# Delta rule with a gated MLP: the state's products woven in pairs, U and S in buffers of their own

## The chip, the cores and the metric

The kernel runs on one core of one Trainium2 chip. The metric is the device time of one execution in microseconds (us); before the change it is 664.31 us, the median of three runs that went from 662.4 to 664.77 us. A difference of less than about 0.5% (3.3 us) can't be told from no change.

## The reference

What is computed, cut to what matters: a linear attention with a state per head, updated token by token by the delta rule, and a spatially gated MLP behind it.

```python
k_n = k / (np.linalg.norm(k, axis=-1, keepdims=True) + 1e-06)
for t in range(S):                       # S = 768; B, H, D = 4, 8, 48
    kt, vt, bt = (k_n[:, :, t], v[:, :, t], beta[:, :, t, None])
    y[:, :, t] = np.einsum('bhd,bhde->bhe', q[:, :, t], state)
    v_old = np.einsum('bhde,bhd->bhe', state, kt)
    state = state + bt[:, :, :, None] * np.einsum('bhd,bhe->bhde', kt, vt - v_old)
...
h = np.maximum(x @ w_in, 0.0)            # x: y as (4, 768, 384); d_ff = 1024
u, v = (h[..., :d_ff // 2], h[..., d_ff // 2:])
v_n = (v - mu) / np.sqrt(var + 1e-06)    # over the last axis
v_s = np.einsum('ts,bsd->btd', w_spatial, v_n) + b_spatial[None, :, None]
return ((u * v_s) @ w_out).astype(np.float32)
```

All matrix products are in float32 or in pairs of rounded halves (`float32r`).

## The kernel before

The sequence of each batch is cut into 12 chunks of 64 tokens. One **step** handles one chunk of one batch with its 8 heads; there are 48 steps. Head h + 2u stands with h = 0 or 1 on one half of the 128 partitions and with u = 0 to 3 along the free axis. Two chains of steps (batches 0 and 2, batches 1 and 3) are interleaved by the list `ORDER`: six steps of the first chain alone, then one of each in turn, then six of the second alone. A step whose chain is also that of the step before it (`late`) is called `solo` in the code.

In each step these groups of small matrix products run on TensorE (8 calls each, 4 u by 2 h; every float32 call shows in the trace as two weight loads and two matmuls):

- **products** (line 359): K times K and K times Q of a later chunk; two VectorE operations (lines 373 and 374) mask them into `ta`. Both use K padded with zeros to 128 rows, so that a call has 128 rows and 64 columns and streams 128 columns. There is one such call group for each of the steps 8 to 47.
- **E** (line 585) and **F** (line 597): the lower left 32 by 32 block of the inverse of a unit triangular matrix, 32 rows by 32 columns, on the diagonal halves of the array (input and output on the same half of the partitions). ScalarE copies the results (lines 588 and 600, one copy for each h). The inverses of the 32 by 32 blocks come from "lanes" (lines 531 to 566), a long chain of VectorE operations for each group of 4 steps.
- **A** (line 642): K times the state S; VectorE adds it to v (line 645). Its operands lie on the half opposite to that of the result.
- **B** (line 659): the inverse times v; VectorE scales it into U, one operation for each h (line 663).
- **C** (line 678): K natural times U; VectorE adds it to S, one operation for each h (line 682).
- **D** (line 692): the output, from S and U in one call of 112 or 128 rows and 64 columns. For this, S and U of a head stand in one buffer `su`, S on one half of the partitions and U on the other, and ScalarE copies the masked K times Q (line 650, `step_k`) beside Q into `kqa`, so that both are one operand.

The groups of a step are issued in three places: `slot_a` (A and F of step s), `slot_cd` (C and D of step `late`, the step before), `slot_b` (B of s, E of s + 1). In each place lie, behind the groups, the products of later steps, some VectorE operations of the lanes (`lane`), pieces of the preparation of weights and norms (`pump`) and `fill(rate)`, which issues matmuls of the MLP worth `rate` us (1.5, from step 18 on 1.7) up to a cap. The groups are issued under a higher priority (`hp()`, 300 instructions ahead). The order on each engine but VectorE in the opening is then found by the tile framework's scheduler, which goes by priority and by when operands are ready and buffers free; PSUM buffers for A to F come from one pool, `pa`, with four.

The MLP (lines 752 to 896) takes products of 128 rows by 128 columns: `mlp_v` (line 759), `mlp_u` (820), `mlp_g` (839), `mlp_o` (884). What is left of it when the steps are over runs at the end by itself.

SyncE issues all DMAs, among them per step `kqa` in two parts (lines 622 and 623), `knat` (617), `v` (612) and the padded `kq` (336).

Of the kernel before, what the change touches and what calls it, by code (L numbers as in the profile page):

```python
# [15 lines left out]
CH = 64  # L16
# [62 lines left out]
def delta_rule_gated_mlp(  # L79
# [3 lines left out]
    kp_t: bass.AP,  # L83
    qb_t: bass.AP,
    qa_t: bass.AP,
    kv_nat: bass.AP,
    b_nat: bass.AP,
# [39 lines left out]
    sus = []  # L127
    for i in range(4):
        su = const.tile([128, 2 * NU * HD + 16], F32, name=f"su{i}")
        nc.gpsimd.memset(su, 0.0)  # L130
        sus.append(su)

    def su_view(t, h, u, rows, w=HD):
        o = (h * NU + u) * HD
        return t[rows, o : o + w]

    def su_all(t, h, rows):
        o = h * NU * HD
        return t[rows, o : o + NU * HD].rearrange("p (u e) -> p u e", e=HD)
# [131 lines left out]
    cn_g, ta_g, ad_g, w_g = {}, {}, {}, {}  # L271

    def group_norm(g):
# [49 lines left out]
        cn_g[g] = cn  # L323
# [3 lines left out]
    def load_kq(s):  # L327
        if s < NST:
            if KQB <= s < 2 * G:
                kq_t_[s] = moe.tile([KR, 2, NU, CH], F32, name="kq", tag="vh", bufs=VB)  # L330
            else:
                kq_t_[s] = work.tile([128, 3, NU, CH], F32, name="kq", bufs=KQB)
            if s < 2 * G:
                nc.sync.dma_start(out=kq_t_[s][0:KR, 0:2], in_=kq_t[s])
            else:
                nc.sync.dma_start(out=kq_t_[s], in_=kp_t[s - 2 * G])
# [11 lines left out]
    def products_mm(s):  # L348
# [7 lines left out]
        p1 = pq.tile([128, 512], F32, name="pq").rearrange("p (u y t) -> p u y t", u=NU, y=2)  # L356
        for u in range(NU):
            for h in range(2):
                nc.tensor.matmul(  # L359
                    p1[rows_t(h), u],  # L360
                    kq[:, h, u, :],
                    kq[:, h : 3 : 2 - h, u, :],
                    start=True,
                    stop=True,
                )
# [4 lines left out]
    def products_out(s, p1):  # L370
        g, sl = divmod(s, G)
        ta = ta_g[g]
        nv.tensor_tensor(out=ta[:, 0, sl], in0=p1[:, :, 0], in1=mcs[s % len(mcs)], op=ALU.mult)
        nv.tensor_tensor(
            out=ta[:, 1, sl], in0=p1[:, :, 1], in1=mpos.unsqueeze(1).broadcast_to([128, NU, CH]), op=ALU.mult
# [201 lines left out]
    def step_e(s):  # L577
        tt, tn = t_of(s), tn_t.pop(s)
        pi = pi_t[s] = work.tile([128, NU, 32], F32, name="pi", bufs=1)
        p2 = pa.tile([128, 512], F32, name="pa")  # L580
        pp = p2[:, : NU * 32].rearrange("p (u c) -> p u c", c=32)
        for u in range(NU):
            for h in range(2):
                r, lo = slice(h * 64, h * 64 + 32), slice(h * 64 + 32, h * 64 + 64)
                nc.tensor.matmul(pp[lo, u], tt[r, u, 32:64], tn[r, u, :], start=True, stop=True)
        for h in range(2):
            lo = slice(h * 64 + 32, h * 64 + 64)
            nc.scalar.copy(out=pi[lo], in_=pp[lo])

    def step_f(s):  # L590
        tt, pi = t_of(s), pi_t.pop(s)
        p3 = pa.tile([128, 512], F32, name="pa")
        px = p3[:, : NU * 32].rearrange("p (u c) -> p u c", c=32)
        for u in range(NU):
            for h in range(2):
                r, lo = slice(h * 64, h * 64 + 32), slice(h * 64 + 32, h * 64 + 64)
                nc.tensor.matmul(px[r, u], pi[lo, u, :], tt[lo, u, 32:64], start=True, stop=True)  # L597
        for h in range(2):
            r = slice(h * 64, h * 64 + 32)
            nc.scalar.copy(out=tt[r, :, 32:64], in_=px[r])  # L600
# [13 lines left out]
    def prefetch_kn(s):  # L614
        if s < NST:
            kn_t[s] = work.tile([128, NU, HD], F32, name="knat", bufs=2)
            nc.sync.dma_start(out=kn_t[s], in_=kv_nat[s, :, 0])

    def prefetch_kq(s):
        if s < NST:  # L620
            kqa = kqa_t[s] = work.tile([128, 3, NU, CH], F32, name="kqa", bufs=2)
            nc.sync.dma_start(out=kqa[0:64, 0:2], in_=qb_t[s])
            nc.sync.dma_start(out=kqa[64:112, 1:3], in_=qa_t[s])

    def step_v(s):
# [5 lines left out]
        if c == 0:  # L631
            nc.gpsimd.memset(sus[2 * ch], 0.0)

    def step_a(s):
        ch, b, c = ORDER[s]
        v, kqa, su = v_t[s], kqa_t[s], sus[2 * ch + c % 2]
        if c == 0:
            return
        pr = psl(pa.tile([128, 512], F32, name="pa"), HD)
        for u in range(NU):  # L640
            for h in range(2):
                nc.tensor.matmul(  # L642
                    pr[rows_t(h), u], kqa[rows_d(h), 1, u, :], su_view(su, h, u, rows_d(h)), start=True, stop=True
                )
        nc.vector.tensor_add(out=v, in0=v, in1=pr)  # L645

    def step_k(s):
        aqk, kqa = t_of(s, 1), kqa_t[s]
        for h in range(2):
            nc.scalar.copy(out=kqa[rows_t(h), 2 - 2 * h], in_=aqk[rows_t(h)])  # L650

    def step_b(s):
        ch, b, c = ORDER[s]
        tt, cn = t_of(s), cn_g[s // G][:, s % G]
        r, su = v_t.pop(s), sus[2 * ch + c % 2]
        pu = psl(pa.tile([128, 512], F32, name="pa"), HD)
        for u in range(NU):
            for h in range(2):
                mark["pb"] = nc.tensor.matmul(  # L659
# [608 lines left out]
```

## Time and profile before

| | |
|---|---|
| median of 3 runs | 664.31 us (662.4 to 664.77) |
| the profiled execution: first to last instruction | 665.8 us |
| TensorE: matmuls / weight loads busy | 564.1 us (85%) / 490.7 us (74%) |
| VectorE / ScalarE / GpSimd busy | 449.3 / 264.3 / 205.0 us |
| mean granted clock of TensorE | 0.885 |
| bytes moved by DMA | 74.63 MB |

The profile has one execution. Its span is 665.8 us, 1.5 us above the median of the runs; no separate time of that execution is given. PE is TensorE's matmuls and PEld its weight loads, which overlap; DVE is VectorE, ACT ScalarE, POOL GpSimd, SPq the queue that issues DMAs. A form such as `48*64 48x48` means weights of 48 rows by 64 columns, and a moving operand of 48 rows by 48 columns. In rows of the timeline, the first number is the start and the second the length of a merged run of instructions, both in us, and xN their number.

### The profile page before, as it was taken

How to read it: one execution, taken by the hardware profiler on the slowest of the kernel's cores; microseconds unless marked ns; L12 is line 12 of the kernel's file. 1: busy time of each engine (PE TensorE's matmuls, PEld its weight loads, DVE VectorE, ACT ScalarE, POOL GpSimd, SP SyncE). 2: the span in 40 equal slices, each digit the busy share in tenths (PEclk: the TensorE clock that was granted, in tenths of full speed). 3: DMA queues.
4: the chain of work that ended last, by engine and by line, in shares of the span. 5: the costliest groups of instructions: out<-in, count | busy, mean ns of one | idle time of the engine just before them, and what ended most of it. 6: DMA issues, size and time to landing. Idle time of an engine off the chain costs nothing.

```text
span 665.8 us, 19042 instructions
## 1 busy us (share of the span) xinstructions
PE 564.1 (85%) x7432; PEld 490.7 (74%) x7432; DVE 449.3 (67%) x1565; ACT 264.3 (40%) x712; POOL 205.0 (31%) x250
## 2 busy tenths in 40 slices
PE   5425758758759797999999899989999999999997
PEld 4324647647648576888878778879898789998997
DVE  3588968999879768788595685799836822223142
ACT  1223233552437254432432646731326574215321
POOL 4114445463324324133322224233213133310000
PEclk9998656955588787889899899998999899999999
DMA  8554386847553563724537436454253231101001
GB/s 235 132 127 131 106 178 202 232 115 186 146 108 109 151 140 89 158 86 112 109 107 187 93 100 172 97 130 94 78 130 84 71 69 42 46 19 36 1 25 48
DMA packets 144522, 74.63 MB, mean 112 GB/s; under 512 B 105136, under 2 KB 128432, under 8 KB 144432
## 3 DMA queue, kind: packets, MB, share of 16 engines
q1 hardware_dynamic: 144432, 73.41, 43.6%
q8 instruction: 59, 0.97, 0.6%
q14 instruction: 31, 0.25, 0.1%
HBM read 58.16 MB, written 14.02 MB: 108 GB/s over the span
## 4 chain that ended last, share of the span: by engine, by line
PE 44%; DVE 13%; DMA 7%; SPq 5%; issue 2%; ACT 2%; POOL 0%; DVEq 0%; ACTq 0%
PE pm L839 11%; PE pm L820 6%; PE pm L884 4%; DVE prod L543 4%; PE pm L759 4%; DVE w L550 4%; PE pa L692 2%; PE pa L659 2%; PE pa L642 2%; PE pq L359 2%; PE pa L678 2%; PE pma L839 2%; DMA kqa<-in_qa_t 2%; PE pa L597 2%; PE pma L884 1%
## 5 line engine op out<-in xcount | busy, mean ns | idle before, releaser
L550 DVE TENSOR_TENSOR w<-w,prod 128x30 f32<-128x30 f32 (+4 forms) x330 | 102.1, 309 | 9.0 <-issue 2.2
L839 PE MATMUL pm<-wsp_h,vh 128*128 128x256 f32 x252 | 74.6, 296 | 0.0
L839 PE MATMUL pm<-wsp_h,vl 128*128 128x256 f32 x252 | 74.6, 296 | 0.0
L359 PE MATMUL pq<-kq 128*64 128x128 f32 x640 | 63.1, 320 | 13.2 <-DVE ta L156 7.6
L839 PE MATMUL pm<-wsp_l,vh 128*128 128x256 f32 x252 | 74.3, 295 | 0.0
L543 DVE TENSOR_TENSOR prod<-w,la 128x30 f32<-128x30 f32 (+8 forms) x180 | 62.6, 348 | 13.0 <-ACT w L522 8.7
L659 PE MATMUL pa<-v,ta 64*64 64x48 f32 x768 | 46.2, 249 | 26.4 <-DVE v L645 12.0
L659 PEld LDWEIGHTS pa<-v,ta 64*64 64x64 f32 x768 | 37.0, 159 | 38.6 <-ACT ta L600 10.9
L359 PEld LDWEIGHTS pq<-kq 128*64 128x64 f32 x640 | 45.5, 160 | 22.7 <-issue 8.5
L628 POOL TENSOR_TENSOR v<-v,cn 128x192 f32<-128x192 f32 x48 | 24.7, 515 | 118.1 <-DMA v<-in_kv_nat 83.4
L543 DVE TENSOR_TENSOR prod<-w,lb 128x120 f32<-128x120 f32 (+3 forms) x150 | 54.4, 363 | 3.8
L839 PEld LDWEIGHTS pm<-wsp_h,vh 128*128 128x128 f32 x252 | 50.0, 199 | 1.4 <-issue 0.7
L600 ACT COPY ta<-pa 32x128 f32<-32x128 f32 x96 | 24.3, 253 | 67.0 <-PE pa L597 65.7
L839 PEld LDWEIGHTS pm<-wsp_h,vl 128*128 128x128 f32 x252 | 49.8, 198 | 1.4 <-issue 0.7
L642 PE MATMUL pa<-su,kqa 48*64 48x48 f32 x704 | 39.2, 239 | 13.6 <-DMA kqa<-in_qa_t 6.6
L839 PEld LDWEIGHTS pm<-wsp_l,vh 128*128 128x128 f32 x252 | 49.9, 198 | 0.9 <-issue 0.2
L663 DVE TENSOR_TENSOR su<-pa,cn 64x192 f32<-64x192 f32 x96 | 33.8, 352 | 22.5 <-PE pa L659 21.3
L341 POOL TENSOR_TENSOR mc<-mpos,cn 128x256 f32<-128x256 f32 x44 | 27.0, 615 | 67.8 <-DVE ta L156 58.3
L642 PEld LDWEIGHTS pa<-su,kqa 48*64 48x64 f32 x704 | 30.9, 149 | 22.2 <-issue 12.8
L682 DVE TENSOR_TENSOR su<-su,pa 48x192 f32<-48x192 f32 x88 | 31.0, 352 | 20.0 <-PE pa L678 18.1
L692 PE MATMUL pa<-kqa,su 128*64 128x64 f32 (+1 forms) x768 | 44.4, 250 | 0.0
L678 PE MATMUL pa<-su,knat 64*48 64x48 f32 x704 | 35.3, 227 | 5.8 <-DVE su L663 5.6
(144 smaller groups left out, 1294.8 us busy)
## 6 DMA issues: line engine op xcount, KB each, us to landing
kq<-in_kp_t SPq DMA_DIRECT2D x40, 384.0 KB, 3.9
ad<-ta SPq DMA_DIRECT2D x24, 256.0 KB, 3.9
kqa<-in_qb_t SPq DMA_DIRECT2D x48, 128.0 KB, 2.7
kqa<-in_qa_t SPq DMA_DIRECT2D x48, 96.0 KB, 2.6
v<-in_kv_nat SPq DMA_DIRECT2D x48, 96.0 KB, 2.3
knat<-in_kv_nat SPq DMA_DIRECT2D x48, 96.0 KB, 2.3
out<-ob SPq DMA_DIRECT2D x24, 192.0 KB, 2.0
kn<-in_kv_nat SPq DMA_DIRECT2D x20, 192.0 KB, 3.4
```

Of the source, the lines that this page charges most:

```text
L359: nc.tensor.matmul(p1[rows_t(h), u], kq[:, h, u, :], kq[:, h : 3 : 2 - h, u, :], start=True, stop=True,)
L543: (nc.gpsimd if PG0 <= g < PG1 else nc.vector).tensor_tensor(out=pr, in0=w[:, :n, j : j + 1].broadcast_to([128, n, m]), in1=(la[:, j, j + ...
L550: nc.vector.tensor_add(out=w[:, :n, j + 1 : 32], in0=w[:, :n, j + 1 : 32], in1=pr)
L642: nc.tensor.matmul(pr[rows_t(h), u], kqa[rows_d(h), 1, u, :], su_view(su, h, u, rows_d(h)), start=True, stop=True)
L659: mark["pb"] = nc.tensor.matmul(pu[rows_t(h), u], tt[rows_t(h), u, :], r[rows_t(h), u, :], start=True, stop=True)
L663: mark["db"] = nc.vector.tensor_tensor(out=su_all(su, h, rows_t(h)), in0=pu[rows_t(h)], in1=cn[rows_t(h), 1].unsqueeze(2).broadcast_to([64 ...
L678: nc.tensor.matmul(ps[rows_d(h), u], kn[rows_t(h), u, :], su_view(su, h, u, rows_t(h)), start=True, stop=True)
L682: nc.vector.tensor_add(out=su_all(nx, h, rows_d(h)), in0=su_all(su, h, rows_d(h)), in1=ps[rows_d(h)])
L692: nc.tensor.matmul(py[rows_t(h), u], su_view(su, h, u, kr, 64), kqa[kr, 2 - 2 * h, u, :], start=True, stop=True)
L820: nc.tensor.matmul(pu[:, k], w[:, kt, d0 : d0 + 128], a[:, kt], start=(n == 0), stop=(n == 3 * NK - 1))
L839: nc.tensor.matmul(p[:, k], v[i][:, d0 : d0 + 128], w[:, si, ts], start=(n == 0), stop=(n == 3 * NT - 1))
L884: nc.tensor.matmul(po[:, :DM], a[:, d, ts], w[:, d], start=(n == 0), stop=(n == 3 * ND - 1))
```

## The change

- **Two places of issue instead of three.** `slot_1` issues A of s woven with C of late, then F of s woven with D of late; `slot_2` issues B of s woven with E of s + 1. "Woven" means that the calls of two groups are listed in turn, one of each. In a solo step, C of late is woven with F of s, and D and A follow alone. `fill` is called twice with 1.5 times the rate instead of three times with the rate.
- **U and S apart.** `su` becomes `sts` and `uts`, and U stands on the half of the partitions opposite to that of v (`rows_s`). For this, K natural (`ks_nat`) comes from memory with its halves exchanged, the masked K times Q is written on the exchanged halves, and the scale `cs` is copied to the exchanged halves by two small DMAs for each group of 4 steps.
- **D in two parts.** S times Q and U times masked K times Q are two accumulating calls of 64 rows and 64 columns instead of one of 112 or 128 rows. `step_k` and its two ScalarE copies go away, and `kqa` holds only K and Q, in one DMA.
- **Evictions.** B and C have one VectorE operation each instead of two.
- **Products.** No padding: 16 calls of 48 rows and 64 columns, streaming 64, instead of 8; K times K and K times Q go to two PSUM buffers.
- E and F keep their shapes, 32 rows by 32 columns.

The core of the diff:

```diff
-        p1 = pq.tile([128, 512], F32, name="pq").rearrange("p (u y t) -> p u y t", u=NU, y=2)
+        p1 = [psl(pq.tile([128, 512], F32, name="pq"), CH) for _ in range(2)]
         for u in range(NU):
-            for h in range(2):
-                nc.tensor.matmul(
-                    p1[rows_t(h), u],
-                    kq[:, h, u, :],
-                    kq[:, h : 3 : 2 - h, u, :],
...
+            for y in range(2):
+                for h in range(2):
+                    nc.tensor.matmul(
+                        p1[y][rows_s(h) if y else rows_t(h), u],
+                        kq[rows_d(h), 0, u, :],
+                        kq[rows_d(h), y, u, :],
...
+    def weave(*lists):
+        for k in range(max(len(x) for x in lists)):
+            for x in lists:
+                if k < len(x):
+                    x[k]()
+
+    UH = [(u, h) for u in range(NU) for h in range(2)]
...
+    def prep_a(s):
...
+            [mm(pr[rows_t(h), u], kqa[rows_d(h), 0, u, :], cols(st, u, rows_d(h))) for u, h in UH],
+            lambda: nc.vector.tensor_add(out=v, in0=v, in1=pr),
...
+    def prep_f(s):
...
+        return [mm(px[half(h, 1), u], pi[half(h, 0), u, :], tt[half(h, 0), u, 32:64]) for u, h in UH], post
...
+    def prep_b(s):
...
+            mark["pb"] = nc.tensor.matmul(
+                pu[rows_s(h), u], tt[rows_t(h), u, :], r[rows_t(h), u, :], start=True, stop=True
+            )
...
+    def prep_c(s):
...
+            [mm(ps[rows_s(h), u], cols(kn, u, rows_s(h), 64), cols(ut, u, rows_s(h))) for u, h in UH],
+            lambda: nc.vector.tensor_add(out=heads(nx, lo), in0=heads(st, lo), in1=ps[lo]),
...
+    def prep_d(s):
...
+            for h in range(2):
+                mms.append(
+                    mm(py[rows_t(h), u], cols(st, u, rows_d(h), 64), kqa[rows_d(h), 1, u, :], stop=False)
+                )
+            for h in range(2):
+                mms.append(
+                    mm(py[rows_t(h), u], cols(ut, u, rows_s(h), 64), aqk[rows_s(h), u, :], start=False)
+                )
...
+    def do(*preps):
+        weave(*(p[0] for p in preps))
+        for p in preps:
+            p[1]()
...
+        def slot_1():
+            with hp():
+                if s == NST or late is None or solo:
+                    if late is not None:
+                        do(prep_c(late), *([prep_f(s)] if s < NST else []))
+                        do(prep_d(late))
+                    elif s < NST:
+                        do(prep_f(s))
+                    if s < NST:
+                        do(prep_a(s))
+                else:
+                    do(prep_a(s), prep_c(late))
+                    do(prep_f(s), prep_d(late))
...
+            fill(1.5 * rate)
...
-        def slot_b():
+        def slot_2():
             with hp():
-                step_b(s)
-                step_k(s)
-                if s + 1 < NST:
-                    step_e(s + 1)
+                do(prep_b(s), *([prep_e(s + 1)] if s + 1 < NST else []))
                 prefetch_v(s + 2)
```

More of the change, by code (lines that the diff above doesn't have):

```diff
@@ new lines, in prep_b, with post, one @@
+    def prep_b(s):
+        ch, b, c = ORDER[s]
+        tt, cs = t_of(s), cs_g[s // G][:, s % G]
+        r, ut = v_t.pop(s), uts[2 * ch + c % 2]
+        pu = psl(pa.tile([128, 512], F32, name="pa"), HD)
+        def post():
+            mark["db"] = nc.vector.tensor_tensor(
+                out=heads(ut), in0=pu, in1=cs.unsqueeze(2).broadcast_to([128, NU, HD]), op=ALU.mult
+            )
+        def one(u, h):
+            mark["pb"] = nc.tensor.matmul(
+                pu[rows_s(h), u], tt[rows_t(h), u, :], r[rows_t(h), u, :], start=True, stop=True
+            )
+        return [lambda u=u, h=h: one(u, h) for u, h in UH], post
@@ new lines, in post @@
+        def post():
+            qt = c % 4
+            if qt == 0:
+                while pend["xs"] > 1:
+                    fill(1.0)
+                    pump()
+                pend["xs"] += 1
+                xs[ch] = moe.tile([128, NU, 256], F32, name="xs")
+            x = xs[ch]
+            nc.scalar.mul(out=x[0:112, :, qt * 64 : qt * 64 + 64], in_=py[0:112], mul=-1.0)
+            if qt == 3:
+                spawn(convert((b * NC_ + c) // 4, x))
+                if CI:
+                    tasks[-1][1] = next(tasks[-1][0])
```

252 lines of the change are left out of this document (85 added, 167 removed).

## The prediction, made before the changed kernel was run

> **What bounds the kernel now.** I read the page first, then the busy time by stretch, then the timeline of the weight loads inside one step.
>
> ```profile
> span 665.8 us, 19042 instructions
> PE 564.1 (85%) x7432; PEld 490.7 (74%) x7432; DVE 449.3 (67%) x1565; ACT 264.3 (40%) x712; POOL 205.0 (31%) x250
> PE   5425758758759797999999899989999999999997
> PEclk9998656955588787889899899998999899999999
> PE 44%; DVE 13%; DMA 7%; SPq 5%; issue 2%; ACT 2%; POOL 0%; DVEq 0%; ACTq 0%
> ```
>
> TensorE is busy for 85% of the span, and in most slices of the second half for 90% or more; the chain that ended last is PE for 44%, DVE for 13%. The steps (those of line 659, 16 matmuls each) divide into two stretches:
>
> ```profile
> 49.00:180.00 131.00, 11.59 (x160) 9.78 (x160) 0.64 0.61 161
> 180.00:588.00 408.00, 34.63 (x608) 27.17 (x608) 0.93 0.43 106
> 50.00:180.00 130.00, 91.41 (x1258) 76.14 (x1254) 113.66 (x380) 49.81 (x144) 60.01 (x75) 0.64 0.61 162
> 180.00:587.00 407.00, 378.19 (x5121) 324.73 (x5122) 281.87 (x1010) 179.19 (x485) 128.58 (x140) 0.93 0.43 106
> ```
>
> The first two rows are line 659 alone: 160 / 16 = 10 steps before 180 us and 608 / 16 = 38 after it. The next two are all engines (PE, PEld, DVE, ACT, POOL, then granted clock). Before 180 us DVE is busy for 113.66 of 130 us, PE for 91.41 at a mean clock of 0.64: DVE is the bound, with 39 us of PE idle. After it PE is busy for 378.19 of 407 us: PE is the bound, 29 us idle, 10.7 us a step. What the change does to PE's time per step counts there nearly in full.
>
> Now one step, seen in the weight loads (start, length, shape, number):
>
> ```profile
> 304.82 0.54 PEld L642 LDWEIGHTS pa<-su,kqa 48*64 48x64 f32 x16
> 305.42 0.33 PEld L597 LDWEIGHTS pa<-ta,pi 32*32 32x32 f32 x16
> 305.79 0.44 PEld L678 LDWEIGHTS pa<-su,knat 64*48 64x48 f32 x16
> 306.28 0.55 PEld L692 LDWEIGHTS pa<-kqa,su 112*64 112x64 f32 x16
> 306.89 0.19 PEld L839 LDWEIGHTS pm<-wsp_l,vh 128*128 128x128 f32 x1
> ...
> 206.35 0.55 PEld L659 LDWEIGHTS pa<-v,ta 64*64 64x64 f32 x16
> 206.95 0.33 PEld L585 LDWEIGHTS pa<-tn,ta 32*32 32x32 f32 x16
> 207.32 0.41 PEld L820 LDWEIGHTS pm<-xh,win_h 128*128 128x128 f32 x3
> ```
>
> From start to next start, A costs 0.60 us, F 0.37, C 0.49, D 0.61, B 0.60, E 0.37: 3.04 us. The groups already lie as A, F, C, D together and B, E together, so two places of issue in place of three change little. Each group's loads end before the next begins. That is not so where the array is divided alike:
>
> ```profile
> 253.35 0.55 PEld L692 LDWEIGHTS pa<-kqa,su 112*64 112x64 f32 x16
> 253.81 1.08 PEld L359 LDWEIGHTS pq<-kq 128*64 128x64 f32 x18
> ```
>
> Here D is followed by products of the same tile size, and their loads begin 0.09 us before D's have ended. Between tiles of different size TensorE empties first.
>
> **The decisive rows.** In one place the scheduler has, by itself, set E (32 by 32, diagonal) and A (64 by 64, opposite diagonal) in turn, call by call, which is what the change writes for F with D and B with E:
>
> ```profile
> 282.72 0.13 PEld L585 LDWEIGHTS pa<-tn,ta 32*32 32x32 f32 x2
> 282.90 0.19 PEld L642 LDWEIGHTS pa<-su,kqa 48*64 48x64 f32 x2
> ...
> 285.80 0.19 PEld L642 LDWEIGHTS pa<-su,kqa 48*64 48x64 f32 x2
> 286.04 0.19 PEld L839 LDWEIGHTS pm<-wsp_h,vl 128*128 128x128 f32 x1
> ```
>
> The eight pairs cost 286.04 - 282.72 = 3.32 us, one 0.415. Apart, the same 16 calls cost 0.37 + 0.60 = 0.97 us. Weaving unlike tile sizes costs 2.35 us per eight pairs.
>
> **The change, part by part, late stretch (38 steps).**
>
> *A with C.* Both are 64 by 64 tiles, on opposite diagonals, so four tiles are in use. Bounds: one group's 0.60 us, and the sum 1.09. How near four tiles come to the lower bound is seen in a group that already uses four:
>
> ```profile
> 43.43 0.30 PEld L487 LDWEIGHTS pa<-ta,prod 32*16 32x16 f32 x32 [0.57 <-ACT prod L481]
> ```
>
> 32 loads in 0.30 us, under 10 ns each, against 16 in 0.33 us for F on two tiles. I take 0.65 us: -0.44 a step. The Trainium skill, "TensorE: Matmul & The Clock Gate", "Wait — 56ns, not 53.3ns?", says that the time from start to start never falls below about 25 ns; by that A with C would be an estimated 0.8 us and the sum 6 us more, but this row speaks against it.
>
> *F with D.* D becomes 16 calls of 64 rows, all on the two tiles of one diagonal. Eight pairs at 0.415 us make 3.32; the eight D calls left over cost as D does now, 0.61. Together 3.93 against 0.37 + 0.61 = 0.98: +2.95 a step. Whether they come out in turn is the scheduler's matter. F waits for E's copies and for the PSUM buffer that B had, D for B's eviction and for the buffer that E had: both are ready on the same two events, so I take this weave as full. Apart, D's 16 further loads would add between C's run of 0.44 and its own of 0.55; with 0.46, D is 1.07 and the bound below +0.46.
>
> *B with E.* B waits for F's two copies, E for the eviction of C before them: E may be ready earlier and go alone. Bounds 0.97 (apart) and 3.32 (woven); I take the middle: +1.18 a step.
>
> Together (-0.44 + 2.95 + 1.18) x 38 = +140 us.
>
> *Products.* Now 16 loads of 128 rows:
>
> ```profile
> 274.72 0.85 PEld L359 LDWEIGHTS pq<-kq 128*64 128x64 f32 x14
> 275.73 0.41 PEld L820 LDWEIGHTS pm<-xh,win_h 128*128 128x128 f32 x3 [0.17 <-ACT pm L779]
> ```
>
> 14 loads take 1.01 us to the next start, 16 some 1.1. After: 16 calls over four tiles, like A with C, all of one size: 0.65. Bounds 0.6 to 1.1. I take -0.45 for each of the 40 groups, about 26 of them late: -12 us.
>
> *Clock.* The granted clock falls after sparse stretches:
>
> ```profile
> 283.40:286.80 3.40, 3.40 (x32) 2.78 (x32) 3.01 (x10) 2.50 (x7) 2.46 (x3) 1.00 0.46 161
> 286.80:290.20 3.40, 3.40 (x18) 2.84 (x18) 3.33 (x8) 0.00 (x0) 1.61 (x2) 0.50 0.36 103
> ```
>
> The first is the woven stretch above, PE without a gap in the trace, and the 3.4 us after it run at 0.50 of the clock. Such a window loses 1.7 us. Every step gets a woven stretch of over 3 us; if each brought a half window, 38 x 1.7 = 65 us. MLP matmuls between them may keep the clock, so the other end is nothing, and I take half: +32. The Trainium skill, "TensorE: Matmul & The Clock Gate", "HAM oscillation — how this bites in real kernels", puts the drop on idle gaps of over about 3.4 us; by that rule there would be none here, and the sum 32 us less. The rows show a drop with no such gap.
>
> *Idle time.* 29 us of PE idle in this stretch wait for DMAs, DVE and ACT, which go on while PE is slower; I take a third as swallowed: -10. Late stretch: 140 - 12 + 32 - 10 = +150 us.
>
> **Early stretch (10 steps, half clock, DVE-bound).**
>
> ```profile
> 227.20 0.17 PEld L597 LDWEIGHTS pa<-ta,pi 32*32 32x32 f32 x2
> 227.44 0.23 PEld L678 LDWEIGHTS pa<-su,knat 64*48 64x48 f32 x2
> 227.76 0.17 PEld L597 LDWEIGHTS pa<-ta,pi 32*32 32x32 f32 x2
> ...
> 260.27 0.93 PEld L692 LDWEIGHTS pa<-kqa,su 128*64 128x64 f32 x14
> 261.32 0.93 PEld L659 LDWEIGHTS pa<-v,ta 64*64 64x64 f32 x16
> 262.34 0.50 PEld L585 LDWEIGHTS pa<-tn,ta 32*32 32x32 f32 x16
> ```
>
> At half clock a pair costs 0.56 us, B 1.02, D 1.05, E 0.50 and what empties after it, some 0.55. F with D: 8 x 0.56 + 1.05 = 5.5 against 1.6, +3.9; B with E, half woven: (4.48 - 1.57) / 2 = +1.45; A with C, at twice the full-clock price, -0.8. That is +4.55 x 10 = 45 us; 14 groups of products give back about 0.8 each, 11. The 34 us left meet 39 us of idle PE; the weaves lie on the path from A to B to C, so I hide half: +17. (In the six solo steps it is C that is woven with F; the price is the pair's.) VectorE gains where it is the bound:
>
> ```profile
> L663 DVE TENSOR_TENSOR su<-pa,cn 64x192 f32<-64x192 f32 x96 | 33.8, 352 | 22.5 <-PE pa L659 21.3
> L645 DVE TENSOR_TENSOR v<-v,pa 128x192 f32<-128x192 f32 x44 | 15.3, 348 | 21.3 <-PE pa L642 20.9
> ```
>
> An operation of 128 by 192 costs 348 ns, one of 64 by 192 costs 352: the merged evictions halve, 0.35 us each for B and C, -0.7 x 10 = -7. In the late stretch this lies beside PE. Early: +10 us.
>
> *Costed at nothing.* The nearest row for a small transfer from SBUF to SBUF (KB each, us to landing) is
>
> ```profile
> xs<-xs SPq DMA_DIRECT2D x72, 16.0 KB, 1.9
> ```
>
> ScalarE's two copies of `step_k` go, on an engine busy for 40%. SP issues one DMA fewer a step (`kqa` in one part) and two small ones more for each group of 4 steps (`cs`). These wait for VectorE's norms, and the loads of K, Q and v queue behind them; norms are made three groups ahead, and if that cover were gone, each of the 12 groups would wait for a landing, 1.9 us: +23 us. A group of products takes both buffers of the pool `pq`, so a second one waits for the two masks of the first, 256 columns each, some 0.47 us by the 348 ns of 192; one group in most steps of 10.7 us hides that, and three in one step would cost under 2 us, 10 times.
>
> **Sum:** +150 + 10 = +160 on the execution of 665.8 us makes 826; the median, 664.3, is 1.5 us less, and so is the forecast, rounded: 825 us.
>
> **Rivals.**
>
> 1. *Both weaves full, and a half window in each step.* Late 38 x (-0.44 + 2.95 + 2.35) = 185, -12 + 65 - 10 = +228; early half of 60 - 11, less 7, +18: 910 us. For it: nothing but the scheduler's order holds B from E, and in the rows of 206 us they follow at once.
> 2. *The groups stay apart*, because the scheduler sends each list when its operands come, F and E ahead. Then the tile sizes change as often as now. Late: (-0.44 + 0.46) x 38 = +1, products -12; early: products -11 and VectorE -7, with half of the former hidden, -13: 640 us, faster. It decides where fewer than about 8 of the 38 late steps weave (24 us against 2.95 each). Against it: F and D wait for the same events, and the rows at 282 us show the scheduler weave two ready groups unasked.
> 3. *Tiles on opposite diagonals run beside each other whatever their size.* Then F hides in D (1.07) and E in B (0.60); 0.65 + 1.07 + 0.60 = 2.32 against 3.04, -27 late, with the products -39; early, at twice the price and half hidden, -12, and VectorE's -7: 606 us. The Trainium skill, "TensorE: Matmul & The Clock Gate", "The mechanism", lets tiles of different rows and columns overlap without a word on unlike sizes; "TensorEngine Tiling (Array Packing)", "Key Properties", says that a change of the tiling mode drains the array. The rows at 282 us are opposite diagonals and did not overlap, so they go with the second page.
>
> **Chances.** The forecast (F with D woven, B with E from nearly none to nearly all) 0.64; rival 1 0.21; rival 2 0.10; rival 3 0.03; no difference 0.02. The forecast's own ends: no B with E and no clock loss, 38 x 2.51 = 95, less 22, and +3 early, 740 us; and nearly rival 1. The range of 715 to 925 takes in rival 1 and leaves out the apart cases. A measurement here tells about 0.5% from no change. Slower 0.86, same 0.02, faster 0.12.
>
> **What would show it.** Right: in the weight loads of the new profile, rows of x2 in turn between the lines of F and D, 0.41 to 0.43 us a pair; A with C in runs of 32 loads under 0.9 us; PE still 90% busy after 180 us, more slices with a clock under 9. Wrong: F and D as runs of x16 and x32 (rival 2), or loads of F begun between D's without gaps (rival 3). What would make the sum wrong though the mechanism is right: the share of steps that weave, and the clock.

## The result, and the profile after

Before: 664.5 us (median of 4 runs, 662.4 to 665.0). After: **1035.5 us** (median of 4, 1027.6 to 1044.0). The ratio is 1.553, 95% interval 1.546 to 1.561. The forecast was 825 us, with a range up to 925: the direction was right, the size was not. The profiled execution of the changed kernel is the longest of the four, of a slower kind that the interval leaves out. Its mean granted clock is 0.657, that of the other three 0.725 to 0.734, for times only 0.6 to 1.6% shorter; what is worked out below from this trace's clock holds for this execution alone.

The page of the changed kernel:

```profile
span 1042.3 us, 21640 instructions
PE 974.6 (94%) x8840; PEld 780.0 (75%) x8840; DVE 408.6 (39%) x1474; ACT 229.3 (22%) x616; POOL 202.1 (19%) x253
...
PEclk8555566556565655655567966755555578988999
...
PE 81%; DVE 7%; DMA 6%; issue 2%; SPq 1%; POOL 1%; ACT 1%; DVEq 0%; POOLq 0%; ACTq 0%
```

PE is busy for 94% and makes up 81% of the chain that ended last (before 85% and 44%). The row of the clock, in which before had 8 and 9 from the middle on, now stands mostly at 5 to 7 until the last fifth. Busy time by stretch (PE, PEld, DVE, ACT, POOL, then granted clock), the second row for the late steps:

```profile
50.00:180.00 130.00, 109.54 (x1285) 89.38 (x1286) 105.32 (x353) 41.66 (x119) 61.54 (x74) 0.55 0.51 129
180.00:940.00 760.00, 750.35 (x6362) 580.31 (x6364) 248.82 (x948) 151.76 (x415) 117.89 (x134) 0.63 0.23 54
```

The steps before ended at 592 us, 38 of them after 180 us; now they end at 953 us, 40 of them after 180 us. From 180 us to the last step is 773 us instead of 412. PE has no gaps to speak of, 9.7 us idle in the 760 of the row, and the clock has gone from 0.93 to 0.63.

What PE does is seen in the weight loads. L673 is B, L634 the helper of A, C, D, E and F (told apart by the tiles), L904 an MLP call:

```profile
499.88 0.18 PEld L634 LDWEIGHTS pa<-ta,pi 32*32 32x32 f32 x2 [0.33 <-issue]
500.12 0.29 PEld L904 LDWEIGHTS pm<-wout_l,gh 128*128 128x128 f32 x1
500.74 0.29 PEld L634 LDWEIGHTS pa<-ta,uts 64*64 64x64 f32 x2 [0.33 <-issue]
501.15 0.29 PEld L904 LDWEIGHTS pm<-wout_h,gl 128*128 128x128 f32 x1
...
508.41 0.13 PEld L634 LDWEIGHTS pa<-tn,ta 32*32 32x32 f32 x2
508.59 0.19 PEld L673 LDWEIGHTS pa<-v,ta 64*64 64x64 f32 x2
508.83 0.13 PEld L634 LDWEIGHTS pa<-tn,ta 32*32 32x32 f32 x2
...
511.32 0.13 PEld L634 LDWEIGHTS pa<-tn,ta 32*32 32x32 f32 x2
511.49 0.31 PEld L634 LDWEIGHTS pa<-sts,kqa 48*64 48x64 f32 x8
...
515.85 0.17 PEld L634 LDWEIGHTS pa<-ta,pi 32*32 32x32 f32 x2
516.09 0.28 PEld L634 LDWEIGHTS pa<-kqa,sts 48*64 48x64 f32 x2
516.49 0.17 PEld L634 LDWEIGHTS pa<-ta,pi 32*32 32x32 f32 x2
```

From 508 us B and E stand in turn throughout, 508.83 - 508.41 = 0.42 us a pair (one call of each, two loads a call) at full clock, as forecast. From 515 us it is F and D, 0.64 us a pair at half clock. The rows from 499 us are what the forecast did not have: single MLP calls of 128 by 128 have slipped between the calls of F and D, two 128-wide loads 1.03 us apart with one call of the state between them.

I count in the loads, in TensorE's order, how often the tile size changes (rows by columns, each 32, 64 or 128): 559 times before, **1759** after. Of these, 613 go to or from a 128 by 128 tile (215 before).

### The profile page after: what moved, and what is told of

Its sections match the earlier page's. It is cut to its first block, busy times and chain, and to the rows that moved or that the text cites. A ratio compares the mean times of both kernels' runs of the same rounds, so it can differ in the third digit from the quotient of the medians.

```text
span 1042.3 us, 21640 instructions
## 1 busy us (share of the span) xinstructions
PE 974.6 (94%) x8840; PEld 780.0 (75%) x8840; DVE 408.6 (39%) x1474; ACT 229.3 (22%) x616; POOL 202.1 (19%) x253
## 4 chain that ended last, share of the span: by engine, by line
PE 81%; DVE 7%; DMA 6%; issue 2%; SPq 1%; POOL 1%; ACT 1%; DVEq 0%; POOLq 0%; ACTq 0%
PE pa L634 32%; PE pm L859 17%; PE pa L673 9%; PE pm L840 7%; PE pm L904 5%; PE pm L779 4%; PE pq L360 4%; DVE w L551 2%; DVE prod L544 1%; DMA wd<-w 1%; DMA kn<-in_kv_nat 1%; PE pma L859 1%; DVE wstage L153 1%; DMA ta<-wd 1%; PE pma L904 1%
## 5 line engine op out<-in xcount | busy, mean ns | idle before, releaser
L673 PE MATMUL pa<-v,ta 64*64 64x48 f32 x768 | 131.5, 291 | 10.7 <-DVE v L644 7.2
L634 PE MATMUL pa<-kqa,sts 48*64 48x64 f32 x768 | 117.4, 299 | 0.0
L673 PEld LDWEIGHTS pa<-v,ta 64*64 64x64 f32 x768 | 86.7, 183 | 35.4 <-issue 21.3
L634 PE MATMUL pa<-ta,uts 64*64 64x64 f32 x768 | 112.5, 299 | 0.0
L634 PE MATMUL pa<-ta,pi 32*32 32x32 f32 x768 | 102.4, 229 | 0.4 <-ACT pi L588 0.3
L634 PE MATMUL pa<-tn,ta 32*32 32x32 f32 x768 | 90.8, 231 | 10.9 <-DVE tn L576 5.6
L634 PEld LDWEIGHTS pa<-kqa,sts 48*64 48x64 f32 x768 | 81.0, 189 | 14.8 <-issue 7.6
L634 PEld LDWEIGHTS pa<-ta,uts 64*64 64x64 f32 x768 | 81.2, 195 | 14.5 <-issue 8.2
L634 PEld LDWEIGHTS pa<-ta,pi 32*32 32x32 f32 x768 | 57.7, 123 | 39.9 <-issue 10.3
L360 PE MATMUL pq<-kq 48*64 48x64 f32 x1280 | 81.4, 302 | 2.5 <-DVE ta L153 2.5
L634 PEld LDWEIGHTS pa<-tn,ta 32*32 32x32 f32 x768 | 52.3, 127 | 39.7 <-issue 8.9
L634 PE MATMUL pa<-uts,knat 64*64 64x48 f32 x704 | 68.3, 280 | 4.2 <-ACT wsp_h L167 2.7
L360 PEld LDWEIGHTS pq<-kq 48*64 48x64 f32 x1280 | 62.3, 195 | 10.9 <-issue 3.5
```

What stands on the lines that cost most here:

```text
L360: nc.tensor.matmul(p1[y][rows_s(h) if y else rows_t(h), u], kq[rows_d(h), 0, u, :], kq[rows_d(h), y, u, :], start=True, stop=True,)
L634: return lambda: nc.tensor.matmul(*a, **dict(dict(start=True, stop=True), **k))
L673: mark["pb"] = nc.tensor.matmul(pu[rows_s(h), u], tt[rows_t(h), u, :], r[rows_t(h), u, :], start=True, stop=True)
```

## The experiments

All are of this kernel or of the one before with a part put in or taken out. They use two quantities: the count of changes of tile size, and the late stretch. "Offset" is the constant `HP`, 300 in both kernels, by which the state's instructions are put ahead of the MLP's.

**Set 1: weave and offset.** T1 says that the changes of tile size do it, T2 that the other parts do, T3 that weaving does even between like tiles.

```diff
 apart: each list issued whole
-        for k in range(max(len(x) for x in lists)):
+        for k in range(0, max(len(x) for x in lists), 99):
             for x in lists:
-                if k < len(x):
-                    x[k]()
+                for f in x[k : k + 99]:
+                    f()
 ef64: E and F as 64 by 64 tiles, zeros beside the 32 by 32 blocks (F's zeroed buffer not shown)
-            mm(pp[lo(h), u], tt[h * 64 : h * 64 + 32, u, 32:64], tn[h * 64 : h * 64 + 32, u, :]) for u, h in UH
+            mm(pp[rows_t(h), u], tt[rows_t(h), u, :], tn[rows_t(h), u, :]) for u, h in UH
...
-        return [mm(px[half(h, 1), u], pi[half(h, 0), u, :], tt[half(h, 0), u, 32:64]) for u, h in UH], post
+        return [mm(px[rows_t(h), u], pi[rows_t(h), u, :], tt[rows_t(h), u, 32:64]) for u, h in UH], post
 hp600, ef64_hp600, apart_hp600
-HP = 300
+HP = 600
```

> The changed kernel with one edit: the two lists of a pair are issued one after the other instead of call by call; everything else of the change stays (U and S apart, D in two parts, unpadded products, two fills). Changes of tile size in the order of TensorE's calls: 559 before the change, 1759 with it, 1044 here (of which 757 to or from the MLP's 128 by 128 tiles). Theory 1 (each change of tile size costs a drain, some 0.16 us at full clock and more at half): 485 more than before the change, so 720 to 790 us. Theory 2 (the cost lies in the other parts of the change: 32 loads in D, products in two buffers, two places of issue): stays above 950 us.

> The changed kernel, woven call by call as in the change, with E and F as 64 by 64 tiles: the inverse's block is padded with zeros that are there already (E) or in a zeroed buffer (F), so that all of A to F have one tile size. The result is the same. 655 changes of tile size are left, nearly all to or from the MLP's tiles. Theory 1 (changes of tile size): 640 to 690 us. Theory 2 (other parts of the change): above 950 us. Theory 3 (weaving itself hurts, because four tiles on both diagonals contend): above 900 us, while the kernel with the lists apart is fast.

> The changed kernel with the priority offset of the step's groups at 600 instructions instead of 300, and nothing else. The weave stays: 1282 changes between 32 and 64 tiles (1146 with the change); but MLP calls no longer slip in between: 181 changes to or from 128 tiles instead of 613. Theory 1: 850 to 920 us, since a good part of what my forecast lacked is the slipped MLP calls. Rival: only the woven 32 and 64 tiles and the clock count, and the slipped calls are nothing; then 1030 us or more.

> Both edits together: E and F as 64 by 64 tiles, woven as in the change, and the priority offset at 600. 187 changes of tile size, against 559 before the change. Theory 1: 372 drains fewer than before the change and a third fewer loads in a row for A with C, B with E: 580 to 630 us, faster than before the change. Theory 2 or 3: above 900 us.

> The changed kernel with the priority offset at 600 and each list issued whole: no weave and few slips of MLP calls, 365 changes of tile size (before 559), all other parts as changed. T1: 630 to 690 us. T2 (the other parts cost the 115 us by which ef64_hp600 stands above before): 770 us or more.

| kernel | us | changes of tile size (with 128) |
|---|---|---|
| changed kernel | 1035.5 | 1759 (613) |
| hp600 | 948.5 | 1463 (181) |
| apart | 947.7 | 1044 (757) |
| ef64 | 905.3 | 655 (647) |
| ef64_hp600 | 779.4 (ratio 1.172, 1.166 to 1.178) | 187 (179) |
| apart_hp600 | 763.7 (ratio 1.147, 1.138 to 1.156) | 365 (161) |

hp600, apart and ef64 were timed once each. None of the five times lies in a range that was expected for it.

The longer offset takes away nearly all slipped MLP calls: with it the changes with a 128-wide tile fall to between 161 and 181. So **the weave costs 948.5 - 763.7 = 185 us where no MLP calls slip in**, and the slips another 87 (woven) or 184 (apart); with the slips left in, the weave costs only 1035.5 - 947.7 = 88. Per change that is 0.17 us for a weave (185 / 1098) and 0.27 to 0.29 for a slip (184 / 679, 126 / 468 for ef64, 87 / 296), the lower clock included. T1 is right in kind about these 272 us. What T3 says of TensorE falls: like tiles woven run beside each other, here F with D at 64 by 64 in ef64_hp600:

```profile
400.14 0.13 PEld L636 LDWEIGHTS pa<-kqa,sts 48*64 48x64 f32 x1
...
400.48 0.15 PEld L636 LDWEIGHTS pa<-ta,uts 64*64 64x64 f32 x2
400.50 0.16 PEld L636 LDWEIGHTS pa<-ta,pi 64*64 64x64 f32 x2
400.54 0.15 PEld L636 LDWEIGHTS pa<-ta,uts 64*64 64x64 f32 x2
...
401.22 0.19 PEld L861 LDWEIGHTS pm<-wsp_h,vl 128*128 128x128 f32 x1
```

48 loads take about 1 us, 0.02 us each. But T1 by itself falls too: apart_hp600 has fewer changes than before and stands 100 us above it. The rest of the study is about these **100 us**.

The late stretch of hp600, then that of apart_hp600:

```profile
180.00:858.00 678.00, 657.48 (x6503) 544.76 (x6502) 252.76 (x951) 152.79 (x418) 122.09 (x137) 0.68 0.25 61
```

```profile
180.00:672.00 492.00, 412.37 (x6308) 366.86 (x6303) 256.06 (x950) 151.17 (x411) 119.42 (x133) 0.78 0.35 83
```

Without the weave PE does less work in this stretch than before: 412.37 us at 0.78 is 322 us of full clock, where before has 378.19 at 0.93, or 352. Part of that is MLP work put off: 619 of 1800 MLP calls are left for after the last step (487 before), which take 91 us instead of 74. Counted to the last step in both (672 and 592 us), the stretch is 80 us longer: PE is idle for 80 us instead of 29, and busy for 29 more because of the lower clock. These 51, 29 and 17 us are the 97 by which the span is longer.

**Set 2: single parts, put into the kernel before, and the places of issue taken back.** The edits are shortened: lines are joined, and the bodies of the slots and the loads of the unpadded `kq` are left out.

```diff
 b_products
-        p1 = pq.tile([128, 512], F32, name="pq").rearrange("p (u y t) -> p u y t", u=NU, y=2)
+        p1 = [psl(pq.tile([128, 512], F32, name="pq"), CH) for _ in range(2)]
...
-                nc.tensor.matmul(p1[rows_t(h), u], kq[:, h, u, :], kq[:, h : 3 : 2 - h, u, :], start=True, stop=True)
+                for y in range(2):
+                    nc.tensor.matmul(p1[y][rows_t(h), u], kq[rows_d(h), 0, u, :], kq[rows_d(h), y, u, :], start=True, stop=True)
 b_padded_two: two buffers and 32 calls, 128 rows
+                    nc.tensor.matmul(p1[y][rows_t(h), u], kq[:, h, u, :], kq[:, 2 if y else h, u, :], start=True, stop=True)
 b_narrow_one: one buffer and 16 calls, 48 rows
+                nc.tensor.matmul(p1[rows_t(h), u], kq[rows_d(h), 0, u, :], kq[rows_d(h), 0:2, u, :], start=True, stop=True)
 b_two_places
-        slot_a(); slot_cd(); slot_b()
+        slot_1(); slot_2()
 three_apart_hp600: apart_hp600 with the places of the kernel before
-        slot_1(); slot_2()
+        slot_a(); slot_cd(); slot_b()
```

> The kernel before with one part of the change alone: the products unpadded, 32 calls of 48 by 64 in two PSUM buffers of the pool pq instead of 16 padded calls in one. Tile sizes change 715 times in TensorE's order (before 559). T1 (only changes of tile size cost): (715 - 559) x about 0.25 us, +40 us at most, some 700 us. T2 in its first form (two buffers for a group, so a second group waits for the masks of the first, and that delays the chain of the lanes): 740 us or more. Both theories wrong: 650 to 670 us.

> The kernel before with another part alone: A, F, C, D issued at one place and B, E at a second, the MLP filled in at 1.5 times the rate at each, the lanes called five times a step and not six. No weave, no other tile. 546 changes of tile size. T1: 664 us within 10. T2 in its second form (the places of issue and fewer calls of the lanes make the chain late): 720 us or more.

> The changed kernel with the priority offset at 600, the lists one after another, and the three places of issue of before (A and F; C and D; B and E; six calls of the lanes a step). 403 changes of tile size. T1: 640 to 690 us. T2 second form: clearly below apart_hp600, by 60 us or more, at 660 to 700 us. If it stays with apart_hp600, the places of issue are not the cause, and products, D in two parts or the operands do it.

> The kernel before with the products still padded to 128 rows, but one call for each of the two results: 32 calls of 128 by 64 in two buffers of pq instead of 16 in one. It has the two buffers and the 32 calls of b_products without its narrow rows. Theory P (two buffers and so the order in time make b_products slow): 750 us or more. Theory N (the 48-row tiles make the granted clock fall, which is the whole of b_products' +122 us): 660 to 690 us at a clock above 0.85.

> The kernel before with 16 product calls in one buffer as before, but on 48 rows instead of 128 (tile 64 by 64, the same number of streamed columns, no zeros multiplied). Tile sizes change 506 times (before 559). Theory N: 740 us or more at a clock under 0.85, as b_products. Theory P: 664 us within 15.

| kernel | us | ratio, 95% interval |
|---|---|---|
| b_products | 788.2 | 1.184, 1.173 to 1.195 |
| b_two_places | 686.6 | 1.031, 1.020 to 1.042 |
| b_padded_two | 690.9 | 1.041, 1.036 to 1.046 |
| b_narrow_one | 691.0 | 1.041, 1.034 to 1.048 |
| three_apart_hp600 | 774.1 | 1.162, 1.154 to 1.171 |

The places of issue are not the 100 us: taking them back gives 774.1, not less than apart_hp600; two places in the kernel before cost 20 us, between the two ranges expected. The products alone cost 122 us. 788.2 lies in the range of T2's first form, but its reason, the two buffers, doesn't hold up: of the theories N and P neither does. Narrow rows cost 27 us, two buffers with 32 calls 27, and both together far more than the sum. Much of it is seen in the loads of b_products (L690 is D, L837 an MLP call):

```profile
409.51 0.29 PEld L837 LDWEIGHTS pm<-wsp_h,vl 128*128 128x128 f32 x1
410.02 0.29 PEld L690 LDWEIGHTS pa<-kqa,su 112*64 112x64 f32 x2 [0.22 <-issue]
410.43 0.29 PEld L837 LDWEIGHTS pm<-wsp_h,vh 128*128 128x128 f32 x1
410.94 0.29 PEld L690 LDWEIGHTS pa<-kqa,su 128*64 128x64 f32 x2 [0.22 <-issue]
411.35 0.29 PEld L837 LDWEIGHTS pm<-wsp_l,vh 128*128 128x128 f32 x1
```

MLP calls now slip between the calls of D, 0.92 us from one to the next. Runs of one or two loads of a tile size fill 110 us of its time after 180 us, against 32 before. Why they slip in is not shown. It is not the number of calls alone: b_padded_two issues the same 32, and has no more such runs (31 us) and no more changes with a 128-wide tile (199, before 215) than the kernel before. The same stretch of time in b_products, then in the kernel before:

```profile
330.00:410.00 80.00, 79.06 (x598) 58.23 (x595) 32.00 (x103) 11.66 (x35) 11.34 (x13) 0.65 0.26 57
```

```profile
330.00:410.00 80.00, 76.90 (x1088) 64.61 (x1086) 57.04 (x203) 38.12 (x102) 23.51 (x28) 0.98 0.47 121
```

PE is equally busy and gets through 598 matmuls instead of 1088. So b_products shows slips as in set 1, but they don't account for all of its loss: it has 192 changes with a 128-wide tile more than before (407 against 215), some 55 us at the 0.27 to 0.29 of set 1. The slips are no share of the 100 us of apart_hp600, which has few. That each other small edit costs 20 to 27 us in the kernel before, whichever it is, suggests that the order the scheduler had found for it is better than those it finds next to it; no run tests that.

**Set 3: padding put back into the changed kernel** (its products as in b_padded_two, with the second result on the other half). Theory N was that narrow rows lower the granted clock.

> The changed kernel with its products padded to 128 rows again (32 calls, two buffers); weaves, priorities and places of issue as changed, 1668 changes of tile size (1759). Theory N: the loss of the narrow products goes, some 120 us or more: 830 to 920 us. Theory P: 1000 us or more. The prediction's own sum, which held the products at -12 us, would be 840 us.

> The changed kernel with E and F in 64 by 64 tiles, the priority offset at 600 and the products padded to 128 rows: woven lists of like tiles, 309 changes of tile size, no narrow products. Theory N: 640 to 690 us, so that it would stand near or under before. Theory P, or a latency that comes from the places of issue: 750 us or more, as ef64_hp600 at 779.

1003.2 us (ratio 1.511, 1.507 to 1.516) and 791.9 us (1.193, 1.173 to 1.213). Both lie in the range of theory P, though b_padded_two puts its two buffers at 27 us. Theory N falls: the padding gives 32 us in the one, for 91 changes of tile size fewer, and nothing in the other (779.4 without it).

**Set 4: late masks.** In the kernel before, each group of four steps starts as soon as its lanes' results land, and after 180 us the lanes of one group start at most 11 us after those of the last have ended. In ef64_hp600, after 180 us, the lanes of a group start 6 to 43 us after those of the last have ended: their transfer waits for the last mask of the products, which comes late on VectorE. The edit moves the products up:

```diff
-                products(t)
-                mask_c(t + 1)
+                with tc.high_priority(offset=HP):
+                    products(t)
+                    mask_c(t + 1)
```

> ef64_hp600 (779.4 us) with one thing changed: the products and their masks are issued with the same priority as the steps, so the last mask of a group comes some 0.75 to 1 group of steps earlier in VectorE's order (for group 10 after 7.75 groups of steps instead of 8.5; before has 7.75). Theory L (the masks, and so the transfer of a group to its lanes, come late, and each group of steps waits for its lanes): 640 to 710 us. Theory C (the granted clock or the places of issue hold it back): 760 us or more.

> apart_hp600 (763.7 us) with the products and their masks at the priority of the steps. Lists one after another, 440 changes of tile size (365 without). Theory L: 660 to 700 us, near before. Theory C: 750 us or more.

> ef64_hp600_early with the lists one after another instead of woven, 215 changes of tile size. If weaving like tiles has a value, it is above ef64_hp600_early, by up to 48 x 0.9 us (A with C 0.44 and F with D 0.37 a step by the prediction's prices), +20 to +45 us. If weaving like tiles is worth nothing on this path: within 15 us of it.

> hp600 (948.5 us, woven, tiles as changed, 1421 changes of tile size) with the products and their masks at the priority of the steps. It stays bound by TensorE: 900 to 950 us by the theory that the drains bound it. Its distance to apart_hp600_early is the price of the weave with the late masks taken away; the prediction's 150 to 160 us would be met between 130 and 200.

820.3 us (ratio 1.234, 1.225 to 1.242), 784.2 (1.179, 1.173 to 1.186), 791.8 (1.191, 1.179 to 1.204) and 930.3 (1.399, 1.379 to 1.419). The first two are slower than without the edit (779.4 and 763.7), so theory L falls, though the masks came earlier as meant. They lie in the range of theory C, which names several causes that these times can't tell apart. The wait for the lanes, in ef64_hp600 the second longest of VectorE, is gone in ef64_hp600_early. Waits of ef64_hp600 (total us, times, longest), then of ef64_hp600_early:

```profile
DVE tn L578 <- DMA ta<-wd: 45.3, 8, 7.7
...
PE pa L636 <- DMA kqa<-in_kq_t: 37.1, 15, 6.2
```

```profile
PE pa L636 <- DMA kqa<-in_kq_t: 66.8, 19, 7.3
```

After 180 us the transfer of the lanes' results is now issued 26 to 60 us ahead of their use, but the steps are no faster: another wait takes the place, that of A for the transfer of `kqa`. Two more things follow. hp600_early less apart_hp600_early, 146 us, is the weave's price once more, in the range expected. And like tiles woven are 28 us slower here than apart (820.3 against 791.8), which neither expectation allowed for: PE's time is not what is short, and what the weave of like tiles costs here is open.

**Set 5: the clock, and a version that should be faster.** hp600_wide is hp600 with E and F streaming each column four times (`.unsqueeze(1).broadcast_to([32, 4, 32])` on the moving operand). b_ef64 is the kernel before with E and F as in ef64.

> hp600 (948.5 us at a mean clock of 0.695) with E and F streaming every column four times, into a PSUM tile four times as wide; the tiles, the weave and the order stay (1441 changes of tile size, 1463 without). It adds 3072 streamed columns a step and takes nothing away. If the granted clock falls because the woven stretch streams few columns in a 3.4 us window (the traces show windows of under 0.45 of their columns followed by half clock, and over 0.55 by full clock), the clock after 180 us rises from 0.68 to 0.80 or more, and the time does not rise by the added columns, or falls: 820 to 950 us. If the drains alone hold it and the clock follows from something else: the clock stays within 0.03, and the time rises by 30 to 100 us.

> The kernel before with E and F in 64 by 64 tiles (zeros in place of what the 32-row tiles left out), so that a step's groups A, F and B, E follow without a change of tile size: 372 changes, before 559. At 0.15 to 0.25 us of drain each on a stretch bound by TensorE: -25 to -45 us, so 620 to 645 us and faster than both kernels. If the order that the scheduler finds is worse by as much as with the other small edits (22 to 27 us each), that takes it back: 640 to 670 us.

hp600_wide: 1149.2 us (ratio 1.731, 1.720 to 1.742), late clock 0.63. Neither expectation was met, and the run can't decide about the clock, since the columns per unit of time did not rise. Its loads:

```profile
504.15 0.28 PEld L687 LDWEIGHTS pa<-v,ta 64*64 64x64 f32 x2 [0.38 <-issue]
504.52 0.17 PEld L640 LDWEIGHTS pa<-tn,ta 32*32 32x32 f32 x2
505.08 0.28 PEld L687 LDWEIGHTS pa<-v,ta 64*64 64x64 f32 x2 [0.38 <-issue]
```

A pair now takes 0.93 us, 0.29 more than a pair at half clock did above. The moving columns streamed went down, not up: 2590 in 3.41 us on average between 180 and 580 us, in hp600 3100.

b_ef64: 687.1 us (4 runs; ratio 1.036, 1.031 to 1.042), slower in spite of 372 changes instead of 559, and above both ranges expected. Its page and its late stretch:

```profile
PE 548.0 (80%) x7432; PEld 485.2 (71%) x7432; DVE 454.4 (67%) x1565; ACT 264.8 (39%) x712; POOL 204.5 (30%) x251
```

```profile
180.00:604.00 424.00, 372.97 (x5269) 325.67 (x5270) 283.58 (x1021) 183.54 (x497) 126.45 (x139) 0.92 0.43 105
```

PE is busy for 16 us less than before, and the span is 16.5 us longer: idle time from 180 us to the last step rises from 29 to 51 us. What the fewer changes gave back, waits took. The steps end at 599 us (592 before), and 563 MLP calls are left for after them (487). None of the versions that ran is faster than the kernel before.

## Why the prediction was wrong, point by point

- **The step that failed: all that the change does beside the weave.** The forecast's rival 2 prices every part but the weave and the clock, at 640 us; weave and clock then bring it to 825, 185 more. Measured in the same order, apart_hp600 is 764, the weave adds 185 and the slipped MLP calls 87. So the 210 us by which the forecast fell short are the other parts, which cost 99 us where it had -24, and the slips, for which neither it nor a rival had a term. Why the other parts cost 99 us stays open (below). The weave is the part that was right.
- **The weave between unlike tiles**: right in mechanism and in the price of a pair, 0.415 us forecast and 0.42 measured at full clock. The trace agrees with the Trainium skill, "TensorEngine Tiling (Array Packing)", "Key Properties", that a change of tiling drains the array: B and E lie on opposite diagonals, and in none of the 1759 places where the tile size changes do the loads on either side overlap. That the total agrees too, 185 for 185, is in part luck. The other two kernels that differ in the weave alone are 146 apart. And from apart_hp600 to hp600, by an estimate from the two late rows above, PE's work rises by some 135 us (at before's clock), the clock takes some 110 more, and idle time gives back 59; the forecast had 32 for the clock and 10 for idle time.
- **The slipped MLP calls** are not the weave's doing: with the lists apart there are more of them (757 changes with a 128-wide tile against 613), and they cost more (184 us against 87). That the longer offset takes them away is shown; why 300 no longer sufficed is not.
- **The clock** is a term that was mis-sized: +32 us forecast, 65 at most. An estimate from the one trace of the changed kernel: 750.35 us at 0.63 would be 508 us at before's 0.93 if all of it scaled; but the woven pairs scale by 0.64 / 0.42 = 1.5 rather than 2, and some 280 of them ran at half clock, about 30 us more. That leaves **130 to 160 us of PE work**, slips included (forecast 140 - 12 = 128), and **210 to 240 us of clock**. I had counted the half-clock window that follows a woven stretch, and not that at half clock the next window, too, streams too little to rise again. The record of the clock is cut into windows of 3.413 us, each at full or at half clock. In all twenty traces, from 50 us to the last step, I count the moving columns of the matmuls that start in each:

| columns in the window | at full clock: the next one drops | at half clock: the next one rises |
|---|---|---|
| under 2700 | 302 of 302 | 0 of 1222 |
| 2700 to 3300 | 66 of 90 | 42 of 332 |
| 3300 to 4500 | 53 of 252 | 362 of 528 |
| over 4500 | 0 of 1104 | 27 of 38 |

  The turn lies near 3300 columns from either side. At half clock that is most of what a window holds: MLP calls of 256 columns, 0.213 us apart, stream 4100. The kernel before streams some 4920 in 3.41 us between 180 and 580 us, the changed one 2470. This is a count, not a trial, and hp600_wide did not raise the columns as it was meant to. The forecast cited the Trainium skill, "TensorE: Matmul & The Clock Gate", "HAM oscillation — how this bites in real kernels", for a drop on idle gaps of over about 3.4 us; here PE was busy for 750 of 760 us at a mean clock of 0.63, so the measurement speaks against gaps as the only cause.
- **Products, -12**: wrong in sign when alone (+122), in part by slips that the forecast did not look for. The serial use of the two buffers, which I had judged hidden, costs 27 us in the kernel before with padded rows, the 16 further calls included.
- **Places of issue, "change little"**: 20 us in the kernel before; in the changed one, going back to three gains nothing.
- **Costed at nothing: the transfers.** Rival 2 had 640 us for the groups apart; apart_hp600 took 764. The waits of TensorE after 180 us in apart_hp600, then before:

```profile
PE pa L634 <- DMA kqa<-in_kq_t: 25.2, 13, 5.1
PE pa L634 <- DVE tn L576: 13.1, 5, 3.8
PE pq L360 <- DVE ta L153: 12.1, 3, 7.4
PE pm L904 <- DVE gt L875: 10.3, 3, 8.2
```

```profile
PE pa L659 <- DVE v L645: 10.3, 5, 5.4
PE pa L642 <- DMA kqa<-in_qa_t: 6.6, 3, 3.6
```

  A waits 25 us for `kqa` where it waited 6.6. SyncE issues that transfer once D of two steps before has let go of its buffer; its own wait for that, after 180 us, went from 14.0 to 49.1 us (apart_hp600, then before):

```profile
SPq L614 <- PE pa L634: 49.1, 23, 6.0
```

```profile
SPq L622 <- PE pa L692: 14.0, 20, 4.1
```

  I had counted its DMAs and not when its buffer comes free. The four waits of PE above are 61 us, and with the clock that follows from an emptier PE they are of the size of the 100 us. That they cause it is argued, not shown: where the wait for the lanes was taken away (set 4) that for `kqa` grew.
- **Idle time swallowed, -10**: 29 us fell to 9.7, so -19.

**What stays open**: what makes up the 100 us of apart_hp600. The number of changes of tile size, the places of issue, the padding of the products and the late masks are not it by themselves: with each set right alone, the time stayed. That several of them hold together isn't ruled out, since one wait took the place of another. Never tried alone are D in two parts, U and S apart with their copied scale, `kqa` in one transfer and the merged evictions. Nor was the kernel before run at an offset of 600, so what the longer offset itself costs isn't known. Open too is how much of the loss the clock causes and how much it only accompanies.

## What to carry to other kernels

Before weaving two groups, count how often the tile size changes in the order in which the scheduler will put TensorE's calls, MLP calls included; unlike tiles should not alternate, and weaving like ones brought nothing here either. After an edit to calls that are held together by a priority, look first for other work that has slipped between them. And do not price a slowdown at the clock of the kernel before: where the granted clock goes with what is streamed, as it did in these traces, ask whether the slower kernel will still stream enough to keep it.

## What the runs showed of the hardware

- A pair of two 32 by 32 and two 64 by 64 loads in turn costs 0.42 us at full clock and 0.61 to 0.64 at half; one 128 by 128 load and two loads of 64 columns in turn cost 0.92 (b_products) to 1.03 us (the changed kernel) at half.
- Four tiles of one size, woven, take 48 loads in about 1 us (ef64_hp600 at 400.14); 16 loads on two tiles take 0.60.
- The granted clock fell with PE busy throughout (750 of 760 us). It went with the columns streamed in its windows of 3.413 us: at full clock over 4500 always kept it and under 2700 always lost it, at half clock under 2700 never regained it, and 389 of 566 half-clock windows with over 3300 were followed by full clock.
- Mean clocks of 0.657 and 0.734 in two executions of one kernel came with times of 1044 and 1028 us. Why the lower clock cost so little there is not known.
